# Factor of batch 1 spread in fp32, last output products in two-bank tiles, copies of q of batch 1 by ScalarE

## The chip, the core and the metric

The kernel runs on one core of one Trainium2 chip. A core has five engines that run their own instruction streams: TensorE (PE, matrix products; its weight loads are shown apart as PEld), VectorE (DVE), ScalarE (ACT), GpSimd (POOL) and SyncE (SP). POOL and SP mostly start transfers here. SBUF is the working memory, PSUM the small memory [...] into which TensorE writes. The metric is the device time of one execution in microseconds (us); a smaller one is better.

## What is computed

Two layers follow each other, for 8 batches of 576 positions:

```
kv  = sum over s of k[b,h,s,:] v[b,h,s,:]          # 64 x 64 for each of 8 heads
o   = q @ kv                                        # 576 x 64 for each head
x   = o / sqrt(mean over the head's 64 of o*o + 1e-6) * g_norm
h   = relu(x @ w_in)                                # 512 -> 1024
c   = conv_w[0]*h[s-1] + conv_w[1]*h[s] + conv_w[2]*h[s+1]
out = (h * sigmoid(c)) @ w_out                      # 1024 -> 512
```

q, k, v, the weights and the output are fp32 in memory; most of the work is in bf16. The factor `1/sqrt(...)` is one number for each batch, head and position, so it has to be *spread* over the 64 partitions of its head before it can multiply `o`.

## The kernel before

**An order written out by hand.** The kernel defines about forty small operations, each a Python function. The string `ORDER` lists calls of them (`hm.1.6` is `hm(1, 6)`), and each engine gets its instructions in exactly that order, each behind the one before it (the loop at the end adds an ordering for every engine). Semaphores between the engines come from the data and the buffers alone. So nothing is scheduled at run time: an engine that waits holds up all that stands behind it in its own stream.

**The operations, by the letters used in the order.** A number after the letters is the batch `b`, or the pair of batches `p`, or the stage of the convolution `c`.

- `Lq`, `Lk`, `Lv`, `Lw`: POOL starts the loads of q, k, v and of `w_out`. `ws`: DVE writes `w_in`, times g_norm, as bf16.
- `qt` (`qs` for batch 0): TensorE transposes q into PSUM; `qc` (`qd`): the copy of it to SBUF as `qT`, 128 x 1152 for half a batch. `kv`, `kvc`: the products k'v and their copies.
- `ot.b.t`: the product `o` of head pair t; `sq`: ScalarE squares it; `oc`: a copy of it in fp32.
- The norm of batch 0 takes another way (`on`, `nl`, `nx`, `mu0`). For the others: `ss` sums the squares, `ln` and `ex` (ScalarE, log then exponential) make the factor `rs` in fp32, 128 x 288. Batch 1 is normed alone, then batches 2 and 3 together, 4 and 5, 6 and 7.
- For batches 1, 2 and 3 the factor is spread by TensorE: `sl` (DVE, four instructions, lines 535 to 538) splits the fp32 factor into bf16 parts that stand in different partitions, and `sp.b.t` multiplies them by a matrix of zeros and ones, `spread` (written by `cs` on DVE), which adds the parts again. `mu.b.t` (DVE) is `o` times the spread factor. For batches 4 to 7 it is spread by transfers over DRAM: `rw`, `rr` (SP) and `mr` (DVE).
- `hm.b.f` (eight products of 128 x 288): one 128-wide slice of `h`; `re`: relu by ScalarE. `cv`, `sv`, `mv`: the convolution of two slices of batch 0 by TensorE. `ta`, `ad`: the convolution by DVE; `sg`: sigmoid by ScalarE; `mg`: h times gate by DVE.
- `om.p.m` (eight products of 128 x 512): 128 rows of the output; `ea`: the copy by ScalarE; `st`: SP stores it.
- `wu.n`, `wa.n`: n products of zeros by zeros that keep TensorE busy.

**PSUM.** Two pools: `ps_a` has three tiles of two banks each (`hm`, `ot`, `qt`, `sp`, `cv`, and the last `om`, which is computed in two halves), `ps_b` two tiles of one bank (`om`, `kv`, `ss`, `wu`). A product waits until the earlier contents of its tile have been read.

**Who copies.** `copy` (line 235) gives a copy to DVE or to ScalarE: `qc` goes to DVE unless its name is in the list `ON_ACT`.

Of the kernel before, what the change touches and what calls it, by code (L numbers as in the profile page):

```python
# [51 lines left out]
FP32 = mybir.dt.float32  # L52
# [10 lines left out]

ONES, KEEP, XB, RD, SQO, PW, ON_ACT, ON_DVE = ({0: (0, 1, 2, 3)}, ((0, 2), (0, 3)), (), (), (), (), ('oc.0.0',), ())

ORDER = """
cvq wu.11 qs.0.0 qd.0.0 cvk kv.0.0.1 kvc.0.0.1.0 kvc.0.0.1.1 cs wa.3 ot.0.0 oc.0.0 qs.0.1 kv.0.1.1 sq.0.0 wa.2
on.0.0 nl.0.0 kvc.0.1.1.1 kvc.0.1.1.0 qd.0.1 qs.0.2 wu.1 kv.0.2.1 qd.0.2 kvc.0.2.1.0 kvc.0.2.1.1 ot.0.1 wu.1  # L70
ot.0.2 sq.0.2 oc.0.1 nx.0.0 sd.0.1 wu.3 on.0.2 nl.0.2 Lq.1 nx.0.2 kv.0.3.1 mu0.0.0 kvc.0.3.1.0 kvc.0.3.1.1
qs.0.3 qd.0.3 on.0.1 nl.0.1 wa.4 ot.0.3 sq.0.3 mu0.0.2 cx cz ws.0 nx.0.1 mu0.0.1 wu.2 on.0.3 nl.0.3 nx.0.3
mu0.0.3 wu.5 hs.0.0 hs.0.1 hm.0.0 hm.0.1 re.0.1 re.0.0 Lk.1.0 Lv.1.0 Lk.1.1 ws.1 hm.0.2 hm.0.3 Lv.1.1 Lw Lq.2
Lk.2.2 re.0.2 ws.2 di.1 hm.0.7 qt.1.0 re.0.7 re.0.3 di.0 hm.0.6 re.0.6 hm.0.4 kv.1.0.2 qc.1.0 kvc.1.0.2.1
kvc.1.0.2.0 cm ta.0.2 re.0.4 hm.0.5 re.0.5 ot.1.1 sq.1.1 oc.1.1 ta.0.3 Lv.2.2 ad.0.1 qt.1.1 ot.1.0 oc.1.0
kv.1.2.2 kvc.1.2.2.1 cv.0.1 kvc.1.2.2.0 ta.0.6 qc.1.1 sq.1.0 ot.1.3 sq.1.3 ot.1.2 ta.0.7 ad.0.3 sq.1.2 wu.4
ss.1 oc.1.3 ln.1 ex.1 ta.0.4 sl.1 cv.0.0 ta.0.5 sv.0.0 sv.0.1 oc.1.2 wu.10 sp.1.0 mu.1.0 sp.1.1 sp.1.3 mu.1.1
mu.1.3 qt.2.1 sp.1.2 mu.1.2 qt.2.0 sg.0.1 sg.0.3 mg.0.3 qc.2.0 ad.0.2 hm.1.6 hm.1.7 re.1.6 qc.2.1 sg.0.2
mg.0.2 hm.1.4 hm.1.5 re.1.7 kv.2.0.4 re.1.5 kvc.2.0.4.0 kvc.2.0.4.1 re.1.4 hm.1.0 mg.0.1 ta.1.6 ta.1.7 mv.0.0
Lq.3 Lk.3.2 Lv.3.2 Lq.4 Lk.4.2 ot.2.3 oc.2.3 sq.2.3 hm.1.3 re.1.3 qt.3.1 re.1.0 ot.2.0 ot.2.1 oc.2.0 oc.2.1  # L80
ad.1.3 qc.3.1 sq.2.0 hm.1.2 ot.2.2 sq.2.1 qt.3.0 oc.2.2 sq.2.2 re.1.2 kv.3.0.4 hm.1.1 kvc.3.0.4.1 kvc.3.0.4.0
ot.3.2 re.1.1 ta.1.4 mv.0.1 ta.1.5 ad.1.2 qc.3.0 ot.3.1 sq.3.2 oc.3.2 sq.3.1 om.0.1 ta.1.2 ot.3.0 Lv.4.2
oc.3.1 ot.3.3 qt.4.1 sq.3.0 ss.2 ta.1.3 ad.1.1 sq.3.3 ss.3 qc.4.1 ea.0.1 ta.1.0 ta.1.1 ln.2 qt.4.0 qc.4.0
om.0.0 ex.2 om.0.3 sl.2 oc.3.3 oc.3.0 ea.0.0 ea.0.3 Lq.5 Lk.5.2 Lv.5.2 Lq.6 sp.2.0 sp.3.2 mu.2.0 sp.2.2 mu.3.2
mu.2.2 kv.4.0.4 sg.1.1 sg.1.3 sp.2.1 sp.2.3 om.0.2 sp.3.0 mu.2.3 mu.2.1 mg.1.1 kvc.4.0.4.1 mu.3.0 sp.3.3
hm.2.0 hm.2.3 sg.1.2 re.2.0 kvc.4.0.4.0 mu.3.3 Lk.6.2 mg.1.3 re.2.3 ea.0.2 sp.3.1 mu.3.1 hm.2.2 mg.1.2 re.2.2
ad.1.0 ot.4.0 sq.4.0 hm.3.2 oc.4.0 qt.5.1 kv.5.0.4 qc.5.1 re.3.2 sg.1.0 hm.3.3 kvc.5.0.4.0 ot.4.3 qt.5.0
re.3.3 ta.2.2 sq.4.3 hm.3.1 Lv.6.2 oc.4.3 kvc.5.0.4.1 mg.1.0 re.3.1 ot.4.1 qc.5.0 sq.4.1 oc.4.1 hm.3.0 hm.2.6
ta.2.3 ad.2.1 Lq.7 ot.5.2 re.3.0 re.2.6 hm.2.1 hm.2.7 oc.5.2 sq.5.2 re.2.1 ot.4.2 re.2.7 hm.3.6 st.0.2 oc.4.2
sq.4.2 hm.3.7 ta.2.0 ta.2.1 re.3.6 re.3.7 ot.5.3 hm.3.5 ot.5.0 sq.5.3 st.0.3 st.0.0 st.0.1 Lk.7.2 Lv.7.2  # L90
oc.5.3 re.3.5 sq.5.0 ss.4 ot.5.1 hm.2.4 sq.5.1 ss.5 oc.5.0 om.0.7 ad.2.0 re.2.4 ta.2.6 ta.2.7 ad.2.3 hm.3.4
ln.3 ex.3 oc.5.1 hm.2.5 re.3.4 rw.3 ea.0.7 re.2.5 st.0.7 qt.6.0 qt.6.1 sg.2.3 rr.4.0 om.0.4 ea.0.4 om.0.8
ea.0.8 ta.2.4 ta.2.5 ad.2.2 qc.6.1 qt.7.1 sg.2.1 kv.6.0.4 om.0.6 mr.4.0 qt.7.0 rr.4.2 qc.6.0 kvc.6.0.4.1
mr.4.2 kvc.6.0.4.0 kv.7.0.4 ea.0.6 rr.4.1 sg.2.2 mr.4.1 qc.7.0 rr.4.3 mr.4.3 qc.7.1 ot.6.2 mg.2.3 rr.5.0
rr.5.3 rr.5.2 mr.5.3 oc.6.2 sq.6.2 om.0.5 mr.5.0 hm.4.0 hm.4.6 sg.2.0 re.4.6 kvc.7.0.4.1 hm.4.7 hm.4.5 re.4.0
ea.0.5 re.4.7 re.4.5 hm.4.1 mr.5.2 rr.5.1 mr.5.1 re.4.1 st.0.5 kvc.7.0.4.0 hm.5.6 st.0.6 mg.2.1 re.5.6 ot.6.0
sq.6.0 hm.5.0 re.5.0 mg.2.2 hm.5.1 st.0.4 oc.6.0 st.0.8 re.5.1 ot.7.3 mg.2.0 ot.7.0 sq.7.3 om.1.0 ot.7.1
oc.7.3 oc.7.0 sq.7.0 ot.6.3 sq.7.1 om.1.5 oc.7.1 ta.3.0 ta.3.1 oc.6.3 ea.1.0 ot.6.1 sq.6.3 hm.5.7 hm.5.4
sq.6.1 re.5.7 ot.7.2 oc.6.1 ad.3.0 ea.1.5 sq.7.2 ss.6 st.1.0 re.5.4 hm.4.4 re.4.4 ss.7 ln.4 ex.4 hm.5.5 hm.5.2
om.1.7 re.5.5 hm.5.3 ta.3.6 ta.3.7 oc.7.2 ad.3.3 ta.3.4 hm.4.3 re.5.2 hm.4.2 om.1.2 sg.3.3 ta.3.5 ad.3.2  # L100
ea.1.7 mg.3.3 rw.4 rr.6.0 rr.6.2 st.1.5 st.1.7 rr.6.3 re.4.2 ta.3.2 re.5.3 om.1.4 ea.1.2 re.4.3 om.1.3 ea.1.4
mr.6.0 ta.3.3 sg.3.0 st.1.4 ea.1.3 mr.6.2 rr.6.1 st.1.3 om.1.8 ea.1.8 sg.3.2 ad.3.1 om.1.1 om.1.6 rr.7.3
rr.7.1 mr.6.3 mr.6.1 mg.3.0 sg.3.1 hm.6.0 hm.6.5 mg.3.2 hm.6.1 re.6.0 ta.4.0 ea.1.1 re.6.1 mr.7.1 rr.7.0
ta.4.1 mg.3.1 re.6.5 hm.6.2 hm.6.4 ad.4.0 mr.7.0 st.1.2 rr.7.2 re.6.2 hm.6.7 re.6.7 hm.6.6 ea.1.6 re.6.4
re.6.6 st.1.1 ta.4.4 st.1.6 hm.6.3 re.6.3 om.2.2 om.2.7 mr.7.3 ta.4.5 mr.7.2 ea.2.7 hm.7.4 sg.4.0 re.7.4
hm.7.2 ad.4.2 sg.4.2 re.7.2 hm.7.0 hm.7.6 re.7.0 ta.4.2 st.1.8 ea.2.2 hm.7.3 st.2.7 re.7.3 st.2.2 re.7.6
hm.7.5 hm.7.7 re.7.5 hm.7.1 mg.4.0 ta.4.3 ad.4.1 ta.4.6 ta.4.7 ad.4.3 om.2.6 ta.5.2 mg.4.2 ta.5.3 ad.5.1
om.2.4 sg.4.1 sg.4.3 ea.2.6 st.2.6 ea.2.4 om.2.3 ea.2.3 sg.5.1 re.7.1 om.2.1 st.2.3 ta.5.4 om.2.8 mg.4.3
ea.2.1 ea.2.8 ta.5.5 mg.4.1 om.3.0 ea.3.0 st.2.1 st.3.0 ad.5.2 sg.5.2 ta.5.0 ta.5.1 ad.5.0 om.2.0 ea.2.0
st.2.4 re.7.7 st.2.0 ta.5.6 ta.5.7 om.3.3 sg.5.0 ea.3.3 om.3.2 mg.5.2 om.2.5 ea.3.2 ad.5.3 sg.5.3 ea.2.5  # L110
mg.5.0 st.3.2 mg.5.1 om.3.1 ea.3.1 st.3.3 st.3.1 mg.5.3 om.3.4 ea.3.4 st.2.5 st.3.4 st.2.8 om.3.8 ea.3.8
st.3.8 om.3.5 ea.3.5 om.3.6 ea.3.6 st.3.6 st.3.5 om.3.7 ea.3.7 st.3.7
"""


# [1 line left out]
def kernel(  # L117
# [25 lines left out]
    consts = pool("consts", 1)  # L143
# [3 lines left out]
    ps_a = pool("ps_a", BUFS["a"], space=PSUM)  # L147
# [5 lines left out]
    def load(name, b, h0=0, n=H):  # L153
        src = {"q": q, "k": k, "v": v}[name]
        if (name, b) not in qkv:
            qkv[name, b] = loads.tile([PS, H, R * D], BF16, name=name + "_sb", bufs=BUFS[name])
        nc.gpsimd.dma_start(  # L157
            out=qkv[name, b][:, h0:h0 + n, :],
            in_=src[b, h0:h0 + n].rearrange("h (p r) d -> p h (r d)", r=R))
# [82 lines left out]
    T = {}  # L242
# [29 lines left out]
    idv = ident.rearrange("p (t g c) -> p t g c", t=NT, g=4)  # L272
# [215 lines left out]
    def rows_of(g):  # L488
        return 32 * len(pairs_of(NORM[g][0]))
# [50 lines left out]
    @op  # L540
    def sp(b, t):
        g = NG[b]
        n = rows_of(g)
        bi = NORM[g].index(b)
        ps = ps_a.tile([P, 2, 512], FP32, name="sp_ps", tag="a")
        T["sp", b, t] = ps
        for e in range(2):
            nc.tensor.matmul(
                ps[:, e, :HS], spread[:n, t * 4 + 2 * bi + e, :, :].rearrange("p i d -> p (i d)"), T["w", g],
                start=True, stop=True)  # L550
# [140 lines left out]
    @op  # L691
    def om(p, m):
        h = T["h", p].rearrange("p f b s -> p f (b s)")
        if f"om.{p}.{m}" == LAST:
            ps = ps_a.tile([P, 2, 512], FP32, name="om2_ps", tag="a")
            parts = [(ps[:, i, :D_model // 2], slice(i * D_model // 2, (i + 1) * D_model // 2)) for i in range(2)]
        else:
            ps = ps_b.tile([P, D_model], FP32, name="om_ps", tag="b")
            parts = [(ps, slice(0, D_model))]
        T["om", p, m] = parts  # L700
        for to, cols in parts:
            for f in range(NF):
                nc.tensor.matmul(to, h[:, f, m * P:(m + 1) * P], w_out_sb[:, f, cols],  # L703
                                 start=(f == 0), stop=(f == NF - 1))
# [37 lines left out]
    for ins in list(nc.cur_bb.bb.instructions):  # L742
        e = ins.engine
# [36 lines left out]
```

## Time and profile before

| | us |
|---|---|
| median of three runs (189.17 to 190.07) | 189.31 |
| the profiled execution | 190.19 |
| span of the profiled execution (first to last instruction) | 187.9 |
| TensorE busy in it, 1787 products | 178.5 (95%) |
| DVE busy, 324 instructions | 159.4 (85%) |
| ACT busy, 233 instructions | 150.2 (80%) |
| POOL busy, 42 instructions | 29.3 (16%) |

Matrix products overlap, so a busy TensorE is not one at its peak; how long a product keeps the next one away is read from the distance of the starts of two neighbours, not from its own duration. Work of one engine hides behind that of another wherever no one waits for it. A line number such as L548 is that of the kernel before, as printed above.

### The profile page before, as it was taken

The page shows a single profiled execution, that of the slowest core. Times are in us where ns is not written, and L with a number is a line of the kernel's source. Part 1 is how long each engine was busy: PE and PEld are TensorE (multiplying, and loading weights), DVE is VectorE, ACT ScalarE, POOL GpSimd, SP SyncE. Part 2 cuts the span into 40 slices and gives each one's busy share as a digit, 9 for nine tenths or more (in the row PEclk, how much of TensorE's full clock was granted, in tenths as well). Part 3 has the DMA queues.
Part 4 walks back from the last instruction along what each step waited for, and adds up shares of the span by engine and source line. Part 5 has one row for each costly group of instructions (what it writes and reads, how often), then busy time and mean ns, then how long its engine had stood idle before and what let it go on. Part 6 is the DMA issues. An engine that isn't in the chain of part 4 may idle for free.

```text
span 187.9 us, 4432 instructions
## 1 busy us (share of the span) xinstructions
PE 178.5 (95%) x1787; PEld 108.0 (57%) x1787; DVE 159.4 (85%) x324; ACT 150.2 (80%) x233; POOL 29.3 (16%) x42
## 2 busy tenths in 40 slices
PE   7899998999899999999999999999999999999991
PEld 2444774566555577765566656664467675444451
DVE  4678599898999899999998899999899999999200
ACT  2449689949999899999999999999977496667431
POOL 7994405013052301400000000000000000000000
PEclk9999999999999999999999999999999999999999
DMA  6999999999999999998366531028485220233454
GB/s 147 183 265 332 203 205 204 206 202 203 204 204 203 207 200 238 265 205 128 118 178 196 198 131 61 0 89 262 161 232 178 98 81 3 108 128 129 166 195 167
DMA packets 30876, 32.35 MB, mean 172 GB/s; under 512 B 1776, under 2 KB 25864, under 8 KB 30856
## 3 DMA queue, kind: packets, MB, share of 16 engines
q0 software_dynamic: 20176, 17.01, 54.6%
q1 hardware_dynamic: 10472, 14.76, 23.2%
q10 hardware_dynamic: 208, 0.29, 0.6%
q8 instruction: 14, 0.23, 0.5%
q14 instruction: 6, 0.05, 0.1%
HBM read 37.24 MB, written 9.73 MB: 250 GB/s over the span
## 4 chain that ended last, share of the span: by engine, by line
PE 47%; ACT 25%; DMA 9%; DVE 8%; SPq 4%; issue 2%; POOL 2%; ACTq 0%; POOLq 0%; DVEq 0%
PE om_ps L703 20%; PE h_ps L595 19%; ACT h L608 7%; DMA rb<-scr 6%; ACT sq L435 6%; ACT o L239 5%; SPq L571 3%; DMA v_sb<-in_v_dram 3%; PE kv_ps L319 2%; DVE h L649 2%; ACT L232 2%; ACT row L710 2%; DVE xT L580 2%; PE qt_ps L361 1%; DVE xT L554 1%
## 5 line engine op out<-in xcount | busy, mean ns | idle before, releaser
L595 PE MATMUL h_ps<-xT,w_in_sb 128*128 128x288 bf16 x512 | 68.4, 286 | 1.7 <-DVE xT L580 0.6
L703 PE MATMUL om_ps<-w_out_sb,h 128*128 128x512 bf16 (+1 forms) x296 | 64.4, 373 | 0.0
L595 PEld LDWEIGHTS <-w_in_sb 128*128 128x128 bf16 x512 | 49.3, 98 | 18.6 <-issue 4.1
L703 PEld LDWEIGHTS <-h 128*128 128x128 bf16 x296 | 28.5, 98 | 31.7 <-DVE h L649 0.3
L608 ACT ACTIVATE h<-h_ps 128x576 bf16<-128x576 f32 x64 | 40.1, 656 | 7.0 <-PE h_ps L595 6.6
L628 DVE TENSOR_SCALAR side<-h,cw 128x576 bf16<-128x576 bf16 (+1 forms) x92 | 38.2, 427 | 1.0
L643 ACT ACTIVATE tap<-tap 128x1152 bf16<-128x1152 bf16 (+1 forms) x23 | 34.1, 1496 | 2.3 <-DVE tap L637 2.3
L710 ACT ACTIVATE row<-om_ps 128x512 f32<-128x512 f32 (+1 forms) x37 | 21.5, 586 | 14.9 <-PE om_ps L703 13.6
L637 DVE TENSOR_TENSOR tap<-tap,side 128x1150 bf16<-128x1150 bf16 (+1 forms) x23 | 22.4, 973 | 0.8
L649 DVE TENSOR_TENSOR h<-h,tap 128x1152 bf16<-128x1152 bf16 (+1 forms) x23 | 21.6, 962 | 0.6 <-ACT tap L643 0.6
L636 DVE TENSOR_TENSOR tap<-tap,side 128x1150 bf16<-128x1150 bf16 (+1 forms) x23 | 22.1, 961 | 0.0
L435 ACT ACTIVATE sq<-o_ps 128x576 bf16<-128x576 f32 x31 | 19.7, 662 | 1.9 <-PE o_ps L393 1.9
L239 ACT ACTIVATE o<-o_ps 128x576 f32<-128x576 f32 x29 | 18.5, 657 | 1.8 <-PE o_ps L393 1.8
L628 DVE TENSOR_SCALAR tap<-h,cw 128x576 bf16<-128x576 bf16 (+1 forms) x46 | 19.3, 421 | 0.0
L580 DVE TENSOR_TENSOR xT<-o,rb 128x576 bf16<-128x576 f32 x16 | 12.0, 755 | 2.2 <-DMA rb<-scr 2.1
L237 DVE COPY qT<-qt_ps 128x1152 bf16<-128x1152 bf16 x14 | 10.5, 753 | 3.0 <-PE qt_ps L361 3.0
L728 PE MATMUL wu_ps<-zeros 128*128 128x512 bf16 x37 | 11.6, 454 | 1.2 <-DVE zeros L184 1.2
L157 POOL DMA_DIRECT2D q_sb<-in_q_dram x10 | 7.6, 756 | 33.1 <-PE qt_ps L361 32.2
L393 PE MATMUL o_ps<-qT,kvbd 128*128 128x512 bf16 x32 | 11.7, 379 | 0.0
L157 POOL DMA_DIRECT2D k_sb<-in_k_dram x11 | 9.1, 828 | 11.7 <-PE kv_ps L319 9.0
L361 PEld LDWEIGHTS <-q_sb 96*64 96x64 bf16 x336 | 8.3, 110 | 3.8 <-issue 3.4
L361 PE MATMUL qt_ps<-ident,q_sb 96*64 96x96 bf16 x336 | 9.6, 207 | 0.5 <-DVE xT L554 0.2
(72 smaller groups left out, 126.6 us busy)
## 6 DMA issues: line engine op xcount, KB each, us to landing
out_dram<-row SPq DMA_DIRECT2D x35, 256.0 KB, 2.3
rb<-scr SPq DMA_DIRECT2D x32, 144.0 KB, 3.5
q_sb<-in_q_dram POOLq DMA_DIRECT2D x7, 576.0 KB, 12.1
k_sb<-in_k_dram POOLq DMA_DIRECT2D x6, 576.0 KB, 11.8
v_sb<-in_v_dram POOLq DMA_DIRECT2D x6, 576.0 KB, 15.2
w_stage<-in_moe_w_in_dram POOLq DMA_DIRECT2D x2, 512.0 KB, 6.7
w_stage<-in_moe_w_in_dram POOLq DMA_DIRECT2D x1, 1024.0 KB, 9.5
w_out_sb<-in_moe_w_out_dram POOLq DMA_DIRECT2D x1, 1024.0 KB, 17.8
```

Source lines behind the costliest of these rows:

```text
L239: nc.scalar.activation(to, fr, AX.Copy)
L361: nc.tensor.transpose(ps[i * D:(i + 1) * D, tt, r * PS:(r + 1) * PS], q_sb[:, 2 * (2 * u + tt) + i, r * D:(r + 1) * D], ident[:PS, :PS])
L435: nc.scalar.activation(to, fr, AX.Square)
L595: nc.tensor.matmul(ps[:, e, :HS], w_in_sb[:, t, f * P:(f + 1) * P], x[:, t, e * HS:(e + 1) * HS], start=(t == 0), stop=(t == NT - 1))
L608: nc.scalar.activation(h_tile(b // 2)[:, f, b % 2, :].rearrange("p (e n) -> p e n", e=2), T["hm", b, f][:, :, :HS], AX.Relu)
L628: nc.vector.tensor_scalar_mul(tap[m][:, f % 2, :, :].rearrange("p b s -> p (b s)"), h_tile(p)[:, f, bs, :].rearrange("p b s -> p (b s)"), ...
L636: nc.vector.tensor_add(tap[:, :, 1:], tap[:, :, 1:], side[:, 0, :, :S - 1])
L637: nc.vector.tensor_add(tap[:, :, :S - 1], tap[:, :, :S - 1], side[:, 1, :, 1:])
L643: nc.scalar.activation(tap, tap, AX.Sigmoid)
L649: nc.vector.tensor_mul(h, h, T["tap", c, j])
L703: nc.tensor.matmul(to, h[:, f, m * P:(m + 1) * P], w_out_sb[:, f, cols], start=(f == 0), stop=(f == NF - 1))
L710: nc.scalar.activation(T["os", p, m][:, cols], fr, AX.Copy)
```

## The change

Three lists and the order change, and two operations follow them.

- Batch 1's factor is no longer split. Its `sl` is gone, and `sp.1.t` multiplies the fp32 factor by an fp32 matrix of zeros and ones, `spread32`, with two fp32 products of 128 x 288 for each t. `spread32` (128 x 1024 fp32) is written by POOL, ahead of the load of `w_out`. Batches 2 and 3 keep the split.
- Eight `om` tiles among the last (of the pairs 2 and 3) go to the pool of two-bank tiles `ps_a` instead of `ps_b`, and use one bank of theirs.
- The two copies of the transposed q of batch 1, `qc.1.0` and `qc.1.1`, go from DVE to ScalarE.
- The order is a new one throughout. There are 26 products of zeros ahead of the first `hs` (32 before) and 17 after it (14 before). All other operations are the same, and the loads stand in the same order on POOL.

```diff
-..., ON_ACT, ON_DVE = (..., ('oc.0.0',), ())
+..., ON_ACT, ON_DVE, F32, OM_A = (..., ('oc.0.0', 'qc.1.0', 'qc.1.1'), (), (1,), ((2, 6), (2, 8), (3, 2), (3, 0), (2, 1), (3, 5), (3, 7), (3, 6)))
...
+    spread32 = consts.tile([P, NT * 2, 2, D], FP32, name="spread32") if F32 else None
+
     @op
     def Lw():
+        if F32:
+            nc.gpsimd.tensor_copy(
+                spread32.rearrange("p (t e) i d -> p t (e i) d", t=NT),
+                idv[:, :, 0, 0:4].unsqueeze(3).to_broadcast([P, NT, 4, D]))
         nc.gpsimd.dma_start(out=w_out_sb, in_=moe_w_out.rearrange("(f p) m -> p f m", p=P))
...
     def sp(b, t):
...
+        if g in F32:
+            for e in range(2):
+                nc.tensor.matmul(
+                    ps[:, e, :HS], spread32[:n, 2 * t + e].rearrange("p i d -> p (i d)"), T["rs", g],
+                    start=True, stop=True)
+            return
...
     def om(p, m):
...
+        elif (p, m) in OM_A:
+            ps = ps_a.tile([P, 2, 512], FP32, name="om2_ps", tag="a")
+            parts = [(ps[:, 0], slice(0, D_model))]
```

The order from the copies of q of batch 1 to its first `hm`, before:

```
qt.1.0 re.0.7 re.0.3 di.0 hm.0.6 re.0.6 hm.0.4 kv.1.0.2 qc.1.0 kvc.1.0.2.1 kvc.1.0.2.0 cm ta.0.2 re.0.4 hm.0.5 re.0.5
ot.1.1 sq.1.1 oc.1.1 ta.0.3 Lv.2.2 ad.0.1 qt.1.1 ot.1.0 oc.1.0 kv.1.2.2 kvc.1.2.2.1 cv.0.1 kvc.1.2.2.0 ta.0.6 qc.1.1
sq.1.0 ot.1.3 sq.1.3 ot.1.2 ta.0.7 ad.0.3 sq.1.2 wu.4 ss.1 oc.1.3 ln.1 ex.1 ta.0.4 sl.1 cv.0.0 ta.0.5 sv.0.0 sv.0.1
oc.1.2 wu.10 sp.1.0 mu.1.0 sp.1.1 sp.1.3 mu.1.1 mu.1.3 qt.2.1 sp.1.2 mu.1.2 qt.2.0 sg.0.1 sg.0.3 mg.0.3 qc.2.0
ad.0.2 hm.1.6
```

and after:

```
hm.0.6 re.0.6 qt.1.1 ta.0.2 qc.1.1 qt.1.0 qc.1.0 re.0.5 wu.2 hm.0.7 kv.1.0.2 cs ta.0.3 ad.0.1 ta.0.6 re.0.7 di.1
hm.0.4 ta.0.7 ad.0.3 kvc.1.0.2.1 kvc.1.0.2.0 re.0.4 wu.4 ot.1.0 oc.1.0 sq.1.0 kv.1.2.2 ot.1.1 kvc.1.2.2.1 kvc.1.2.2.0
sq.1.1 wu.4 ot.1.2 ta.0.4 sq.1.2 ot.1.3 sq.1.3 wu.5 ss.1 oc.1.2 oc.1.3 cv.0.1 ln.1 ex.1 ta.0.5 ad.0.2 wu.2 sp.1.3
mu.1.3 oc.1.1 sp.1.0 mu.1.0 sv.0.1 cv.0.0 sp.1.1 sp.1.2 mu.1.1 sg.0.3 sv.0.0 mu.1.2 sg.0.2 qt.2.0 qt.2.1 mv.0.0
qc.2.1 qc.2.0 hm.1.2
```

The writing of the bf16 matrix, `cs` (three DVE instructions, L276 to L278), stands in the start before and among the convolution of batch 0 after. The first `om` stands behind all of `hm.1` before (`om.0.1`), and after it (`om.0.3`) between `ot.2.2` and `oc.2.2`, ahead of `hm.1.5`.

## The prediction

> **What bounds the kernel now.** I read the page first, then the table by stages, then TensorE's timeline, and last the waits. The page puts PE at 95%, DVE at 85% and ACT at 80% of the span, an average that says little. The table below cuts the time from TensorE's first `hm` product (18.03) to its last, at the first `hm` of batch 1, just after the last of them (55.10, in the first `om`), and at the starts of `hm.4.0` and `hm.6.0`. Columns: stretch, length, then busy time (and count) of PE, PEld, DVE, ACT, POOL, the granted clock, DMA share, GB/s.
>
> ```profile
> 18.03:39.20 21.17, 20.07 (x260) 13.17 (x259) 17.13 (x40) 18.02 (x34) 4.46 (x5) 1.00 1.29 204
> 39.20:55.10 15.90, 14.91 (x226) 10.22 (x227) 15.23 (x33) 13.01 (x24) 4.74 (x6) 1.00 1.32 204
> 55.10:101.34 46.24, 45.88 (x650) 29.84 (x648) 43.63 (x70) 45.28 (x69) 5.09 (x6) 1.00 1.05 195
> 101.34:136.38 35.04, 34.66 (x231) 20.56 (x230) 33.25 (x47) 34.22 (x51) 0.00 (x0) 1.00 0.39 131
> 136.38:184.03 47.65, 47.22 (x281) 27.26 (x279) 37.98 (x80) 29.75 (x44) 0.00 (x0) 1.00 0.37 131
> ```
>
> TensorE is nearly full in every row, ACT too from 55 to 136 (79.5 of 81.3 us), DVE in the second row. In the last row only TensorE is. So the end is TensorE's work plus its stalls, and ACT decides in the middle. Real stalls come from distances of starts, in TensorE's timeline around batch 1's factor (start, length, instruction):
>
> ```profile
> 32.34 0.43 PE L500 MATMUL ss_ps<-sq,sel 128*32 128x288 bf16 x8
> 32.85 0.90 PE L670 MATMUL cv_ps<-h,dg 128*128 128x288 bf16 x6
> 33.59 2.32 PE L728 MATMUL wu_ps<-zeros 128*128 128x512 bf16 x10
> 35.81 1.49 PE L548 MATMUL sp_ps<-wparts,spread 128*128 128x288 bf16 x6
> ...
> 39.20 1.14 PE L595 MATMUL h_ps<-xT,w_in_sb 128*128 128x288 bf16 x8
> ...
> 148.23 8.12 PE L595 MATMUL h_ps<-xT,w_in_sb 128*128 128x288 bf16 x64
> 156.18 27.81 PE L703 MATMUL om_ps<-w_out_sb,h 128*128 128x512 bf16 x136
> ```
>
> The unstalled spacing is 0.124 us for 128 x 288 ((156.18 - 148.23)/64) and 0.216 for 128 x 512 (a tile of eight takes 1.73; the fifteen whole tiles and two halves of the last row make 27.7 of its 27.81, so the end has no stall). With these spacings the first stretch is 13.5 us of useful products, 1.0 of `sp.1`, 3.0 of zeros (14 x 0.216) and 3.7 of stalls; the second has 2.8 us of stalls, the third 2.9, the fourth 1.4, the last 0.7. Some 0.1 us at each change of kind is in these and stays.
>
> The ten products of zeros stand where TensorE waits for the split on DVE:
>
> ```profile
> 33.83 0.31 DVE L535 CAST hi<-rs 128x288 bf16<-128x288 f32 x1 [0.39 <-ACT rs L526]
> 34.17 0.52 DVE L536 SCALAR_TENSOR_TENSOR rs<-hi,na,rs 128x288 f32<-128x288 bf16 x1
> 34.73 0.31 DVE L537 CAST hi<-rs 128x288 bf16<-128x288 f32 x1
> 35.08 0.52 DVE L538 SCALAR_TENSOR_TENSOR wparts<-hi,nb,rs 128x288 bf16<-128x288 bf16 x1
> ```
>
> From `rs` (33.79) to `wparts` (35.60) 1.8 us pass: that is the wait to be removed.
>
> [...] No fp32 product of this size is in the trace (the one transpose, L260, is 25 columns). [...] The trace has one case, 133 ns for L260's weights against 98 for bf16 ones. [...]
>
> **The change, part by part.**
>
> *fp32 products.* [...] With 0.05 us left open for each, 4.4: I take +3.4. [...] `mu.1` on DVE (0.75 each, 3.0 in all) no longer paces them.
>
> *Split.* Four DVE instructions, 1.66 us busy, are gone. Before, TensorE reached `sp` at 35.81.
>
> *Copies of q.* Two DVE copies of 753 ns leave; ACT gets two of 128 x 1152 out of PSUM. No row shows this; 128 x 576 copies follow each other at 0.545 (two in 1.09 in the chain), the 1152-wide sigmoid takes 1.16. I take 1.1 each, 2.2 (2.1 to 2.4). What stands behind them on ACT is `re.0.5`, `re.0.7`, `di.1`, the `kvc` and all squares, so `ss.1` waits for them. From `re.0.6` (TensorE, with six `hm.0` done, releases it at about 24.1) ACT then has 4 relus, 4 squares and 3 copies (11 x 0.545 = 6.0), four `kvc` (4 x 0.275 = 1.1), `di.1` (0.98), the two copies (2.2) and `ln`, `ex` (1.0): 11.3, ending at 35.4. So `sp.1.3` starts at 35.4, 0.4 earlier than before, although the split is gone: ACT's new work takes its place.
>
> *Sum of the first stretch after.* 13.5 useful + 4.4 + zeros 17 x 0.216 = 3.7 + stalls. The walk (`sp.1.3` 35.4; two `sp`, `cv.0.0` 0.73, two `sp`: 40.5; `mu.1.2` done at 41.4) gives `hm.1.2` at about 41.6: stalls of 2.0 instead of 3.7. Net +2.4 on 39.20.
>
> *Zeros ahead of `hs`.* Six fewer, 1.3 us; worth nothing, because this stretch follows the loads: the chain has 5.34 us of the load of v, up to 11.03. `cs` (1.58 us of DVE) leaves the start: there it stood while TensorE waited for v until 8.93. It goes to where DVE has 17.13 of 21.17 busy. If that cover were gone it would cost 1.6.
>
> *POOL's copy.* 128 x 1024 fp32, an estimate of 1 to 1.5 us, ahead of the loads of `w_out` and of q, k, v of batch 2. POOL waits 32.2 us in all for `qt`; `w_out` landed at 32.9 (15.08 + 17.8) and is first read at 53.85; v of batch 2 landed at 41.8 (22.65 + 19.1) and is first read at 43.73, so 2 us are to spare. Hidden; without that margin it would be 1 to 1.5 us on TensorE. [...]
>
> *Order from 39 to 55.* Before, TensorE lost 2.8 us here to ACT and to tiles, with nothing else to issue. After, `om.0.3` (1.73 us, one `ps_b` tile) stands among `hm.1`, between `ot.2.2` and `ot.2.0`, where ACT has to read several tiles. I count 1.6 back of 2.8. So at 55 TensorE is +0.8, with DVE 3.2 us lighter (1.66 + 1.51) and ACT level (its free 2.9 us of this stretch absorb the copies).
>
> *From 55 on.* The same operations in another order. In the chain before, the first `rr.4` waited behind a store (`st.0.7`, for an `ea`), and `hm.6.0` waited 0.56 for `mr`. After, `rr.6.3` still stands behind `st.1.4` on SP, behind a sigmoid of ACT; TensorE arrives there later and so waits less: -0.4. Everything else I put at even.
>
> *Two-bank tiles.* The last 27.81 us held no stall, so they can remove none: 0. An `om` in `ps_a` occupies a tile for 1.73 + 0.6; at worst it delays one `hm.7` by 0.3.
>
> Sum: +2.4 - 1.6 - 0.4 = +0.4. Against the profiled execution, 190.19 (span 187.9 and 2.3 around it), that is 190.6; on the median, 189.31, it is 189.7. Half a per cent of this kernel, 0.95 us, is about what a measurement can tell from no change; the forecast is inside it.
>
> **Rivals.**
>
> 1. *The stalls go (faster).* DVE is 3.2 us lighter just where it held 15.23 of 15.90, and an order around that may pack TensorE closer. If the second stretch gets back 2.1 of 2.8, the third 1.2 of 2.9 and the rest 0.6 of 2.1, the sum is 2.4 - 2.1 - 1.2 - 0.6 = -1.5: 187.8. For it: every one of these stalls is short and has a filler somewhere. Against it: from 55 to 136 ACT is 98% full, and the new order gives it no less to do.
>
> 2. *The fp32 products cost more (slower).* Place: the four `sp.1` tiles, with nothing else for TensorE but `cv.0.0`. [...] 1.7 more than assumed: +2.1, 191.4[...]. It decides from about 0.62 us a product on (+0.95 = 0.4 + 8 x 0.07). [...] Against: weight loads of the bf16 products hide behind the one before.
>
> 3. *ACT is the bound (slower).* The copies' 2.2 us shift all of ACT up to 121, where its Ln of batches 6 and 7 starts, and with it `rr.6` and `hm.6.0`. ACT has 2.9 us free in the second stretch, which speaks against it; if half of that can't be used, +1.1 on top: 190.8.
>
> 4. *It does nothing of what it says:* the split was hidden by zeros and other products anyway. That is already in the forecast; the result is the same time.
>
> **How the numbers follow.** Forecast 0.34, rival 1 0.30, rival 2 0.22, rival 3 0.14. The likeliest case alone holds 188.9 to 190.4. The range goes from rival 1's 187.8 to 192.2, which holds rival 3 and rival 2 up to products of 0.8 us (0.4 + 8 x 0.25 = 2.4 on 189.31 is 191.7, with 0.5 for the rest); beyond it and below 187.8 lie 2 in 10. Faster by over 0.5%: 0.30. Slower: most of rival 2, half of rival 3 and a little of the forecast, 0.34. Within: 0.36.
>
> **What would show it.** In the timeline after: starts of neighbouring `sp.1` products 0.5 to 0.6 apart ([...]over 0.62: rival 2); `sp.1.3` at about 35.4 with ACT unbroken before it; `hm.1.2` at about 41.6; ACT's 1152-wide copies at 1.1; POOL's copy under 1.5 and no later k or v wait on TensorE. In the table by stages: stalls of about 1 us instead of 2.8 in the stretch of `hm.1` (less than 0.7 there and less than 2 up to `hm.4.0`: rival 1); ACT's free time from 55 to `hm.6.0` (1.8 us before; rival 3 is right if it stays near that and the stretch still begins late). The prediction is wrong if TensorE's distance from `hm.4.0` to the end, 82.7 us, changes by over 1 us, since I put the late order at even.

## The result and the profile after

| | before | after |
|---|---|---|
| median (6 executions of each, on one chip) | 189.69 | 191.85 |
| lowest to highest | 188.82 to 190.48 | 191.20 to 193.26 |
| the profiled execution | 190.19 | 192.28 |
| its span | 187.9 | 190.4 |

The ratio is 1.0126, with a 95% interval of 1.0086 to 1.0167: slower by about 2.4 us; the medians differ by 2.2. (A ratio is taken from the executions within 1.5% of a kernel's fastest one and is not the quotient of the medians, here 1.0114, which are of all executions.) The forecast was +0.4 us, inside what can't be told from no change. The value lies in the predicted range, and the forecast itself was wrong. That it lies in the range is luck: the upper end, 192.2, was drawn for dearer fp32 products or a late ScalarE, and what was missed lies elsewhere.

The table by stages of the kernel after, cut at the same places as that of before (first `hm`; first `hm` of batch 1; last `hm` of batch 1; `hm.4.0`; `hm.6.0`; end of TensorE's work). Columns as before: stretch, length, busy time (and count) of PE, PEld, DVE, ACT, POOL, granted clock, DMA share, GB/s.

```profile
19.12:42.60 23.48, 22.93 (x270) 15.32 (x268) 17.39 (x35) 20.10 (x36) 4.18 (x5) 1.00 1.30 204
42.60:56.23 13.63, 13.63 (x229) 10.09 (x226) 13.15 (x31) 11.55 (x21) 3.69 (x5) 1.00 1.31 203
56.23:103.24 47.01, 46.18 (x652) 30.05 (x651) 43.90 (x71) 46.21 (x70) 5.68 (x8) 1.00 0.98 182
103.24:138.81 35.57, 34.46 (x231) 20.67 (x230) 33.56 (x47) 34.15 (x51) 0.00 (x0) 1.00 0.43 138
138.81:186.13 47.32, 47.12 (x281) 27.18 (x279) 37.38 (x80) 29.67 (x44) 0.00 (x0) 1.00 0.37 135
```

The second and third rows don't hold the same products in both kernels, because `om.0.3` has moved; together they do. So the 2.5 us between the spans are split like this (distances of starts, from TensorE's timelines):

| | before | after | difference | predicted |
|---|---|---|---|---|
| start to the first `hm` | 18.03 | 19.12 | +1.09 | 0 |
| to the first `hm` of batch 1 | 21.17 | 23.48 | +2.31 | +2.4 |
| to `hm.4.0` | 62.14 | 60.64 | -1.50 | -1.6 |
| to `hm.6.0` | 35.04 | 35.57 | +0.53 | 0 |
| to the end of TensorE's work | 47.65 | 47.32 | -0.33 | -0.4 |
| last copies and stores | 3.85 | 4.31 | +0.46 | 0 |

Three rows are right to 0.1 us, and two are not: the start, and the stretch from `hm.4.0` to `hm.6.0`. (The -0.4 of the prediction is a wait at the third product of `hm.6.0`, so it belongs to the row that begins with this tile.) Without the last row the differences make +2.1, and by this much the two profiled executions differ in time (192.28 - 190.19): about the forecast's +0.4 and the two misses, +1.09 and +0.53.

The last row is in the span and not in the time. It comes with the fp32 products: from TensorE's last product to the end of the span pass 4.3 us in the kernel after and in experiments 1 and 3, which have them, and 3.9 us in the profiles of all other kernels. But the time exceeds the span by 1.8 to 1.9 us in these three and by 2.3 in the others. The reason is not shown.

**The start.** The table by stages again, for 8 to 17 us, of the kernel after:

```profile
8.00:11.00 3.00, 2.01 (x31) 0.88 (x29) 1.50 (x5) 1.18 (x2) 2.65 (x5) 1.00 1.25 182
11.00:14.00 3.00, 2.05 (x42) 1.27 (x43) 2.83 (x9) 2.65 (x5) 2.78 (x5) 1.00 1.17 307
14.00:17.00 3.00, 3.00 (x10) 0.92 (x7) 1.83 (x6) 1.31 (x2) 2.37 (x4) 0.50 1.03 366
```

and of the kernel before:

```profile
8.00:11.00 3.00, 2.27 (x42) 1.28 (x41) 2.50 (x5) 1.93 (x3) 3.00 (x4) 1.00 1.28 191
11.00:14.00 3.00, 2.74 (x44) 1.39 (x46) 2.15 (x5) 1.45 (x3) 3.00 (x6) 1.00 1.14 299
```

The numbers to look at are the one behind the comma (TensorE's busy time) and the third from the end (granted clock). With six products of zeros fewer ahead of the first `hm`, TensorE is busy for 2.0 of 3 us in two stretches, and then its clock is granted at 0.50 for the third; before, it is 1.00 there too. What that does to it is in TensorE's timeline of the kernel after:

```profile
14.24 2.34 PE L746 MATMUL wu_ps<-zeros 128*128 128x512 bf16 x5
16.37 0.26 PE L401 MATMUL o_ps<-qT,kvbd 128*128 128x64 bf16 x1
```

Five products of zeros take 2.13 us from their first to the next instruction; the five at 18.04 in the same kernel take 1.08. Up to there the kernel after isn't late: the last product k'v of batch 0, `kv.0.3`, starts at 13.54, and at 13.60 before. The dip isn't in every execution: four of the six of the kernel after have a mean clock of 0.978 to 0.991 and a median of 192.3 us, the two others (0.996 and 1.00) took 191.3 and 191.4. So +1.09 is what it cost in the profiled one.

**The factor of batch 1.** TensorE's timeline of the kernel after (an fp32 product is recorded as two pairs of weight load and matmul, so x8 are four products):

```profile
36.57 2.18 PE L558 MATMUL sp_ps<-rs,spread 128*128 128x288 f32 x8 [0.17 <-ACT rs L535]
38.69 0.90 PE L685 MATMUL cv_ps<-h,dg 128*128 128x288 bf16 x6
39.43 2.10 PE L558 MATMUL sp_ps<-rs,spread 128*128 128x288 f32 x8
...
42.60 3.11 PE L610 MATMUL h_ps<-xT,w_in_sb 128*128 128x288 bf16 x24
```

The eight products take 2.12 + 2.03 = 4.15 us, 0.52 each. They start 17.45 us after the first `hm` and as soon as ACT has the factor (`[0.17 <-ACT rs L535]`). The four lines of the split on DVE are gone from this stretch.

**From `hm.4.0` to `hm.6.0`.** The factors of batches 4 and 5 come by sixteen transfers (`rr.4`, `rr.5`) that SP issues behind the one that writes the factor (`rw.3`, `scr<-rs`). SP's timeline before:

```profile
89.13 0.33 SPq L562 DMA_DIRECT2D scr<-rs  x1
90.70 0.34 SPq L721 DMA_DIRECT2D out_dram<-row  x1
91.13 12.61 SPq L571 DMA_DIRECT2D rb<-scr  x16
```

and after:

```profile
91.03 0.33 SPq L577 DMA_DIRECT2D scr<-rs  x1
91.39 2.09 SPq L739 DMA_DIRECT2D out_dram<-row  x2
93.58 6.24 SPq L586 DMA_DIRECT2D rb<-scr  x8
99.92 0.54 SPq L739 DMA_DIRECT2D out_dram<-row  x1
100.56 5.98 SPq L586 DMA_DIRECT2D rb<-scr  x8
```

Before, one store stands between `rw.3` and the sixteen, which then follow in a row; the last is issued 14.6 us after `rw.3` has begun (103.74 - 89.13). After, two stores stand ahead of them and a third (`st.0.4`) between, and the last is issued 15.5 us after `rw.3` (106.54 - 91.03). DVE's timeline after shows the `mr` of batch 5 waiting for these transfers, where before the waits are 0.41 and 0.22, and TensorE's shows who pays; before, the same tile, `hm.5.6`, waits 0.19:

```profile
107.83 0.76 DVE L595 TENSOR_TENSOR xT<-o,rb 128x576 bf16<-128x576 f32 x1 [0.68 <-DMA rb<-scr]
109.57 1.43 DVE L595 TENSOR_TENSOR xT<-o,rb 128x576 bf16<-128x576 f32 x2 [0.98 <-DMA rb<-scr]
```

```profile
110.38 2.13 PE L610 MATMUL h_ps<-xT,w_in_sb 128*128 128x288 bf16 x16 [0.64 <-DVE xT L595]
```

This is no chance of one execution. In the experiments below the way from `hm.4.0` to `hm.6.0` takes 35.2 to 35.9 us in the profiles of 1, 2, 5, 6 and 10, which have this late order, and 34.6 to 35.0 in those of 3, 4, 7, 8 and 9, which have that of before.

### The profile page after: what moved, and what is told of

The parts are those of the page before. It is cut to its first block, busy times and chain, and to the rows that moved or that the text cites. A ratio compares the mean times of both kernels' runs of the same rounds, so it can differ in the third digit from the quotient of the medians.

```text
span 190.4 us, 4444 instructions
## 1 busy us (share of the span) xinstructions
PE 180.3 (95%) x1792; PEld 110.3 (58%) x1792; DVE 156.9 (82%) x318; ACT 151.6 (80%) x235; POOL 28.8 (15%) x43
## 4 chain that ended last, share of the span: by engine, by line
PE 41%; DVE 27%; ACT 17%; DMA 5%; POOL 3%; issue 2%; SPq 2%; DVEq 0%; ACTq 0%; POOLq 0%
PE h_ps L610 18%; PE om_ps L721 15%; DVE side L643 7%; DVE tap L652 5%; DVE h L664 4%; DVE tap L651 4%; DVE tap L643 3%; DMA v_sb<-in_v_dram 3%; ACT sq L444 3%; ACT tap L658 3%; ACT h L623 3%; ACT o L241 3%; PE sp_ps L558 2%; PE wu_ps L746 2%; DMA rb<-scr 2%
## 5 line engine op out<-in xcount | busy, mean ns | idle before, releaser
L610 PE MATMUL h_ps<-xT,w_in_sb 128*128 128x288 bf16 x512 | 66.9, 286 | 1.0 <-DVE xT L595 0.6
L728 ACT ACTIVATE row<-om_ps 128x512 f32<-128x512 f32 (+1 forms) x37 | 21.0, 586 | 12.1 <-PE om_ps L721 10.3
L746 PE MATMUL wu_ps<-zeros 128*128 128x512 bf16 x42 | 14.4, 477 | 1.2 <-DVE zeros L186 1.2
L569 DVE TENSOR_TENSOR xT<-o,sp_ps 128x576 bf16<-128x576 f32 x12 | 8.7, 750 | 4.1 <-PE sp_ps L558 3.3
L159 POOL DMA_DIRECT2D k_sb<-in_k_dram x11 | 8.4, 763 | 15.7 <-PE kv_ps L328 11.8
L239 DVE COPY qT<-qt_ps 128x1152 bf16<-128x1152 bf16 x12 | 8.9, 751 | 1.2 <-PE qt_ps L370 1.1
## 6 DMA issues: line engine op xcount, KB each, us to landing
w_out_sb<-in_moe_w_out_dram POOLq DMA_DIRECT2D x1, 1024.0 KB, 18.6
```

The lines of the kernel that those rows point to most:

```text
L610: nc.tensor.matmul(ps[:, e, :HS], w_in_sb[:, t, f * P:(f + 1) * P], x[:, t, e * HS:(e + 1) * HS], start=(t == 0), stop=(t == NT - 1))
L728: nc.scalar.activation(T["os", p, m][:, cols], fr, AX.Copy)
L746: nc.tensor.matmul(ps, zeros[:, 0, :], zeros.rearrange("p t c -> p (t c)"), start=True, stop=True)
```

## The experiments

My theory after the result: the loss has two main parts, a start in which TensorE's clock falls, which the prediction had at nothing, and fp32 products that cost more than the split that they replace, which it had in its sum. The rivals: the copies on ACT, the two-bank tiles, or the order itself. All were timed in five rounds beside the kernel before. Line numbers in these kernels differ by a few from those printed above.

**1. More zeros at the start of the kernel after** (eight products of 128 x 512).

```diff
-... wu.1 kv.0.1.1 ... wu.1 kv.0.2.1 ... ot.0.2 on.0.1 sq.0.2 ...
+... wu.4 kv.0.1.1 ... wu.3 kv.0.2.1 ... ot.0.2 wu.1 on.0.1 wu.2 sq.0.2 ...
```

> The changed kernel with eight more products of zeros ahead of the first hm: wu.4 and wu.3 instead of two wu.1, a wu.1 before and a wu.2 after on.0.1, all where TensorE waits for loads or copies. Nothing else differs. Theory 'clock': the change took six zeros from the start, TensorE's clock fell to half between about 14 and 17 us (the five zeros of wu.5 took 2.13 us instead of 1.08), and all behind it is 1.1 us late; with the zeros back wu.5 takes 1.1, the first hm starts near 18.0 instead of 19.12, and the time falls by 0.8 to 1.2 us, to about 0.5 to 0.7% above the kernel before. Theory 'fp32': the start is no matter, later stalls absorb it, and the time stays within 0.3 us of the changed kernel, 1.1 to 1.3% above before.

Measured: 191.02 us, ratio to before 1.0071 [1.0041, 1.0101], where the unchanged kernel after has 1.0126. TensorE is busy for 3.00 and 2.77 us of the two stretches, the clock stays at 1.00, from 14 to 17 us too:

```profile
8.00:11.00 3.00, 3.00 (x48) 1.39 (x45) 1.84 (x5) 1.79 (x3) 3.00 (x5) 1.00 1.30 193
11.00:14.00 3.00, 2.77 (x44) 1.33 (x37) 2.79 (x11) 2.50 (x5) 3.00 (x6) 1.00 1.14 325
```

The first `hm` is at 17.38 instead of 19.12, and `hm.4.0` and `hm.6.0` are still 1.3 and 1.5 earlier than in the kernel after. None of the eight executions has a mean clock under 0.994. So about 0.55 percentage points of the 1.26% are the start (an estimate from the two intervals: 0.05 to 1.05), and eight products that compute nothing (1.7 us of TensorE) win them back. Not all of it is the clock: 17.38 is also earlier than the 18.03 of before. In the profiles of experiments 5, 6 and 10, which have the same start, the first `hm` comes at 17.8 to 18.1.

**2. The split back in the kernel after**, directly behind the convolution `ad.0.2` on DVE.

```diff
-F32 = (1,)
+F32 = ()
-... ln.1 ex.1 ta.0.5 ad.0.2 wu.2 sp.1.3 ...
+... ln.1 ex.1 ta.0.5 ad.0.2 sl.1 wu.2 sp.1.3 ...
```

> The changed kernel with batch 1's factor split again (sl.1 on DVE behind ad.0.2, bf16 products by spread, no spread32 on POOL), all else as changed. Theory 'fp32': the eight fp32 products cost 8 x (0.52 - 0.124) = 3.2 us of TensorE; the split costs 1.75 us of waiting and the four mu then pace the stage (3.0 us), so the first hm of batch 1 starts 0.5 us earlier and TensorE has the rest as stalls: the time falls by 0.5 to 1 us. Theory 'clock': the start is as cold as in the changed kernel, the first hm still near 19.1, and at most 0.5 us is gained: still 1% above before.

Measured: 191.44 us, 1.0050 [1.0015, 1.0085]. In its profiled execution the clock is at 0.50 from 11.8 to 18.6 us, and again from 39.1 to 42.5, right behind 1.87 us in which TensorE waits for the split, so its stages are not compared; experiment 5 has them. The three of its ten executions with the lowest mean clock (0.968 to 0.973) took 193.0 to 193.4 us, the three with the highest (0.997 to 0.999) 189.5 to 190.4; over all ten the quotient of the medians is 1.007.

**3. The fp32 products alone in the kernel before** (no `sl.1`; its order else kept, the ten zeros `wu.10` too; `spread32` on POOL comes with them).

```diff
-F32 = ()
+F32 = (1,)
-... ta.0.4 sl.1 cv.0.0 ta.0.5 ...
+... ta.0.4 cv.0.0 ta.0.5 ...
```

> The kernel before with the fp32 spread of batch 1 alone: no sl.1, spread32 on POOL, its own order otherwise, wu.10 kept. In that order the first sp waits for sv.0.0 to release its tile at 35.7, so removing the split frees nothing. Theory 'fp32': sp.1 still starts at 35.8, the stage takes 4 x 1.04 and two qt instead of 3.4 us, and the time rises by 1.5 to 2 us (0.8 to 1.1%). If the products hide behind mu: less than 0.5 us.

Measured: 192.84 us, 1.0162 [1.0133, 1.0190], the most expensive single part by far. TensorE's timeline:

```profile
34.33 2.32 PE L742 MATMUL wu_ps<-zeros 128*128 128x512 bf16 x10
36.64 3.15 PE L554 MATMUL sp_ps<-rs,spread 128*128 128x288 f32 x12
```

and ACT's, at the same time:

```profile
34.09 0.44 ACT L531 ACTIVATE rs<-rs 128x288 f32<-128x288 f32 x1
34.55 1.28 ACT L230 ACT_TABLE_LOAD   x1
35.84 1.19 ACT L689 ACTIVATE sq<-cv_ps 128x576 bf16<-128x576 f32 x2
```

The factor is there at 34.53, yet the first `sp` starts at 36.64 and not earlier than before (35.81), for two reasons that don't need the split: TensorE has the zeros until 36.5, and the PSUM tile that `sp` takes is that of `cv.0.0`, which ACT reads behind its table load (the first of the two sigmoids ends at about 36.5). In this order the split was hidden completely. So taking it away brings nothing, the products cost their 3.1 us more, and the first `hm` of batch 1 is 3.3 later (42.50, 39.20 before).

**4. The copies of q of batch 1 on ACT, alone in the kernel before.**

```diff
-ON_ACT = ('oc.0.0',)
+ON_ACT = ('oc.0.0', 'qc.1.0', 'qc.1.1')
```

> The kernel before with the two copies of q of batch 1 given to ScalarE and nothing else. Theory 'clock' and 'fp32': ScalarE has 3 us free between 18 and 39 us, DVE gains 1.5: within 0.5 us of before. Theory 'ACT': the copies stand ahead of the squares of batch 1, so its factor and all of ScalarE come 1 to 2 us later: 0.5 to 1% slower.

Measured: 190.91 us, 1.0063 [1.0042, 1.0083]. ACT's timeline has the copy at its price, and TensorE's the wait behind it:

```profile
30.76 1.11 ACT L237 ACTIVATE qT<-qt_ps 128x1152 bf16<-128x1152 bf16 x1
```

```profile
31.92 0.19 PE L397 MATMUL o_ps<-qT,kvbd 128*128 128x64 bf16 x1 [1.22 <-ACT qT L237]
```

Everything from `ss.1` (33.66, 32.34 before) to the first `hm` of batch 1 (40.52, 39.20) is 1.3 later: ACT paces this stretch, and two copies of 1.1 us stand in the way of the squares.

**5. Both: more zeros at the start, and the split instead of fp32, in the kernel after.**

> The changed kernel with both repairs: the eight zeros at the start and the bf16 split of batch 1's factor. If the cold start and the fp32 products are two separate costs, their gains add: 1.26% less 0.55 less 0.76 leaves the kernel at about the time of before (-0.2 to +0.3%). If both are absorbed by the same later stall, it stays near the better of the two alone, +0.5%.

Measured: 190.57 us, 1.0023 [0.9992, 1.0053]. With the warm start the split is 0.48 points better than fp32 (1.0071), without it 0.76 (1.0126 to 1.0050). That the two gains add up fits their intervals, which are wide: each of these differences is uncertain by 0.4 to 0.5 (estimated from the intervals). What is left over the kernel before, 0.23%, can't be told from zero. It stands for the new order, the copies on ACT and the two-bank tiles together.

**6. The same with the copies of q back on DVE.**

```diff
-ON_ACT = ('oc.0.0', 'qc.1.0', 'qc.1.1')
+ON_ACT = ('oc.0.0',)
```

> As after_warm_split, and the two copies of q of batch 1 on DVE again; what is left of the change is the order and the two-bank tiles. Theory 'ACT': ScalarE's chain to the factor (measured 25.8 to 36.4 us without a gap) gets 2.1 us shorter, the first sp comes 1 to 2 us earlier, and the time falls by 0.5 to 1 us below after_warm_split, below the kernel before. Otherwise within 0.3 us of after_warm_split.

Measured: 193.36 us, 1.0161 [1.0132, 1.0191], 1.4% above experiment 5. The expectation that ACT's relief helps fell. The order is written for a DVE without these copies: DVE is now late with the convolution, and the split stands behind it. DVE's timeline, and TensorE's:

```profile
37.03 0.30 DVE L540 CAST hi<-rs 128x288 bf16<-128x288 f32 x1
```

```profile
38.84 1.14 PE L559 MATMUL sp_ps<-wparts,spread 128*128 128x288 bf16 x4 [3.85 <-DVE wparts L543]
```

The factor was ready at 35.02, the split began at 37.03, and TensorE stood still for 3.85 us (1.87 in experiment 5). Behind this wait its clock fell too, as the table by stages shows:

```profile
38.80:42.21 3.41, 3.37 (x14) 1.93 (x14) 1.61 (x3) 0.75 (x2) 0.00 (x0) 0.50 1.32 203
```

Counted from the first `hm`, the first `sp` comes 1.3 us later than in experiment 5, and from there to the first `hm` of batch 1 it takes 4.64 us instead of 3.49: nearly half of this loss falls into the dip. All five executions have a mean clock of 0.982 to 0.991. So in the order of after the copies on ACT are needed, although in that of before they cost 0.63%.

**7. The two-bank tiles alone in the kernel before.**

```diff
-OM_A = ()
+OM_A = ((2, 6), (2, 8), (3, 2), (3, 0), (2, 1), (3, 5), (3, 7), (3, 6))
```

> The kernel before with the eight last output tiles in two-bank tiles and nothing else. All theories: its last 27.7 us hold no stall, so the time stays within 0.3% of before; over 0.5% slower would mean that the h products of batch 7 wait for these tiles.

Measured: 190.56 us, 1.0025 [1.0002, 1.0048]. No gain, at most half a per cent lost. TensorE's timeline shows one new stall, 0.60 us at 163.19: an `om` that waits until ACT has read the tile of an `hm`.

**8. The kernel before with 26 zeros ahead of the first `hs`** (the first part of an `hm` of batch 0), as in the kernel after.

```diff
-... wa.3 ... wa.2 ... wu.3 ... wa.4 ...
+... wa.1 ... wa.1 ... wu.1 ... wa.3 ...
```

> The kernel before with 26 instead of 32 zeros ahead of the first hm (wa.1, wa.1, wu.1 and wa.3 for wa.3, wa.2, wu.3 and wa.4). Theory 'clock': TensorE's clock drops between 10 and 18 us in at least some executions, the first hm starts up to 1 us later, and the time rises by 0.3 to 0.6%. Otherwise, as the prediction had it: no difference.

Measured: 190.27 us, 1.0009 [0.9981, 1.0036], no difference in the median. The profiled execution (191.54) shows the same dip, earlier and longer, in its table by stages (0.69 from 8 to 11 us, then):

```profile
11.00:14.00 3.00, 2.94 (x31) 1.51 (x28) 1.67 (x5) 0.60 (x1) 3.00 (x5) 0.50 1.11 300
```

Its first `hm` is at 19.77. The median hides that there are two kinds of executions. Eight of the 14 have a mean clock of 0.972 to 0.991 and a median of 191.3 us; the six others (0.996 to 1.00) have one of 189.8. Of the 43 executions of the kernel before beside them only three are at 0.991 or under. So six zeros fewer, with nothing else changed, make the dip frequent, and where it comes it costs about 1.5 us; they don't decide whether it comes.

**9. The start of the kernel after, warm, in front of the order of before.** This was meant as a version that beats both. `cs`, the writing of the bf16 matrix, has to go behind the copies `kvc.1.0.2`.

> The kernel before (split on DVE, copies on DVE, its own order from the first hs on), but with the start of the kernel after and its warm zeros ahead of hs; the writing of the bf16 matrix, cs, moves behind the copies kvc.1.0.2. Theory that the start is a term of its own which is carried to the end: the first hs at 17.4 instead of 18.03, first hm of batch 1 at about 38.6 to 39.0, the time 0.2 to 0.4% under that of the kernel before. Rival, that cs costs 1.58 us once it has left the start, where DVE then holds the split up: first hm of batch 1 at 39.5 to 40.3, the time 0.2 to 0.7% above it.

Measured: 190.45 us, 1.0055 [1.0031, 1.0079]. The rival was right. DVE's timeline:

```profile
25.22 1.23 DVE L276 COPY spread<-bg 128x2048 bf16<-128x2048 bf16 x1
...
34.73 0.30 DVE L540 CAST hi<-rs 128x288 bf16<-128x288 f32 x1
```

`cs` pushes the convolution from 24.99 to 26.36 and the split from 33.83 to 34.73; the first `hm` of batch 1 comes at 40.03 instead of 39.20, although the first `hm` of all was 0.23 earlier. In the kernel after, `cs` stands in the same place, and the copies of q have left DVE there: experiment 6, where they come back, speaks for the two moves belonging together. The warm start gains little here, since half of `hm.0` waits for the last part of `w_in` (0.42 at 22.30).

**10. The split earlier on DVE, ahead of the convolution `ta.0.5`, `ad.0.2`,** in the kernel of experiment 5.

```diff
-... ex.1 ta.0.5 ad.0.2 sl.1 wu.2 ...
+... ex.1 sl.1 ta.0.5 ad.0.2 wu.2 ...
```

> The kernel after with the warm start and the split on DVE directly behind the exponential, ahead of the convolution of batch 0 (ta.0.5 and ad.0.2), instead of behind it. Theory that the split is cheap where DVE is free when the factor is ready: the split's wparts at 1.8 to 2.3 us behind rs, first sp product at about 37.0, first hm of batch 1 at 39.8 to 40.3 (41.3 with fp32), the time 0.3 to 0.6% under the one with the warm start and the fp32 products. Rival, that the convolution is then late and stops batch 0's part: the gain of the first hm is lost by the first hm of batch 2 and the time is the same.

Measured: 192.18 us, 1.0115 [1.0070, 1.0159]. Both expectations fell. DVE's timeline:

```profile
35.46 0.31 DVE L540 CAST hi<-rs 128x288 bf16<-128x288 f32 x1 [3.50 <-ACT rs L531]
...
39.44 2.74 DVE L565 TENSOR_TENSOR xT<-o,sp_ps 128x576 bf16<-128x576 f32 x4
```

DVE has waited 3.50 us for the factor with the convolution behind the split; then the convolution stands ahead of the `mu.1`, which begin at 39.44 (38.26 in experiment 5). From the first `hm` of all to the first of batch 1 it is 24.41 us, 23.21 in experiment 5. The place of four short instructions in DVE's order is worth 1.2 us.

**11. The late order alone:** the kernel before up to `hm.4.0`, then the order of after, with the two-bank tiles.

> The kernel before up to the first product of hm.4.0, and from there the order of the kernel after (with its two-bank tiles; split on DVE and copies of q on DVE as before). Theory that the late order itself is worse by what the two profiles show from hm.4.0 on (+0.5 up to hm.6.0, -0.3 after it): hm.4.0 at 101.3, hm.6.0 at 136.6 to 137.0, the time 0.1 to 0.3% above the kernel before. Rival, that the late order is as good and the kernel after lost 0.5 us there only because its transfers of the factor (rr.4, rr.5) start later against hm.4.0 than before: hm.6.0 at 136.0 to 136.5, the time within 0.1% of the kernel before or under it.

Measured: 190.75 us, 1.0054 [1.0024, 1.0085], above both expectations. The seam between the orders costs by itself: `ot.7.0` follows its copies at once and waits 1.32 us for them, so that `hm.4.0` is at 102.60. Behind it the late order isn't slower: 34.46 us to `hm.6.0` (35.04 before, 35.57 after; one `ot`, about 0.25 us, less stands in this stretch) and 45.03 from there to the end of the next-to-last output tile (45.70 and 45.41). Here the transfers begin as early as before (SP issues fourteen in a row from 90.67), and `hm.5.6` and the `om` behind the gate don't wait; a wait of 0.64 for ACT stands ahead of them instead. That speaks for the late transfers and against the order of the products, but since TensorE comes 1.3 later, it also waits less: the run doesn't settle it.

**12. The kernel of experiment 5 up to `hm.4.0`, then the order of before.**

> The kernel after with the warm start and the split on DVE behind ad.0.2, up to hm.4.0, and from there the order of the kernel before (one-bank tiles). Theory that the late order is worse in itself: 0.1 to 0.3% under the same kernel with the late order of after (which took 1.0023 of the time before), so between 0.9990 and 1.0015. Rival, that the late start of the transfers rr.4 and rr.5 decides, which this kernel keeps: no gain, 1.002 or more.

Measured: 197.60 us, 1.0421 [1.0372, 1.0470]. It tells nothing of the late order: at the seam TensorE waits 2.76 us for the copies ahead of `ot.6.2`, then has its clock at 0.50 from 105.6 to 109.1, and six of the transfers `rr.5` stand behind a store, with DVE idle for 4.30 us for what they bring.

Both runs were badly made in this respect: the order was cut where the two halves hold different operations in flight, and TensorE waited 1.32 and 2.76 us at the seams.

## Where the prediction was right and where it was wrong, step by step

**fp32 products: right.** Predicted 0.55 us each, measured 0.52, which is 4.2 times the 0.124 of a bf16 product of the same size. The 0.55 was the author's estimate: nothing in the profile of before shows an fp32 product of this size. Rival 2 needed 0.62.

**Split, copies, walk to the first `hm` of batch 1: right.** `sp.1.3` was put 17.4 us behind the first `hm` and came at 17.45; the stretch was put 2.4 longer and is 2.31 longer. ACT's copies were put at 1.1 each, and two took 2.15. That ACT's new work takes the place of the split is in the trace after (the products start 0.17 behind the factor, with ACT unbroken from 25.20 on); that the copies on ACT delay this stretch was tested in the order of before only (experiment 4, +1.3 us).

**Zeros ahead of `hs`, "worth nothing": wrong, and the largest miss.** I looked at what the zeros delay and not at what they keep up. The stretch follows the loads only as long as TensorE runs at its full clock: from 14.24 us to the first `hm` TensorE's timeline of the kernel after shows no wait. Its clock there was 0.50 over the whole of 14 to 17 us and 0.94 in the three after it. From 8 to 14 us, ahead of the dip, TensorE was busy for 68% of the time; in experiment 1, where it was busy for 96%, the clock stayed at 1.00. By what rule the clock falls is not shown. Term predicted 0; measured +1.09 in the profile, 0.55 points between experiment 1 and the kernel after. That fewer zeros bring the dip is shown by experiments 1 and 8: it is in none of eight executions with eight zeros more, and the mean clock is low in eight of 14 of the kernel before with six fewer.

**Order from 39 to 55, -1.6, and from there even: the sum right, the parts not.** At `ss.2` the kernel after has done one output tile (1.73 us) more, so 17.33 - 1.73 = 15.60 stand against 17.75: 2.15 came back. Up to `hm.4.0`, 0.65 of it was lost again, among it waits of 0.26 at `hm.2.0` and 0.28 at `sp.3.0`. That the sum comes out at -1.5 is in part luck.

**"After, `rr.6.3` still stands behind `st.1.4` ...: -0.4": right; "Everything else I put at even": wrong.** The 0.56 at `hm.6.0` did go, and for the reason given: the last transfer that it needs is issued at 133.8 in both profiles, and TensorE arrives at 138.81 instead of 136.38. But I followed one of the groups of transfers only. `rr.4` and `rr.5` have two stores ahead of them, where before there was one, and one in their middle, and the wait is now at `hm.5.6`, the first of batch 5 (0.64 for 0.19), with 0.37 at an `om` behind the gate: +0.53 instead of 0. That `hm.5.6` waits for these transfers is in the trace. That the stores are the cause was argued from SP's timelines, and experiment 11 supports it without settling it.

**POOL's copy: right in size (1.05 us for 1 to 1.5, the author's estimate, as the profile of before has no such copy) and hidden.** One DVE instruction took longer beside it, as the timelines of POOL and DVE of the kernel after show:

```profile
14.36 1.05 POOL L306 CAST spread<-ident 128x1024 f32<-128x1024 bf16 x1
```

```profile
12.67 0.74 DVE L489 TENSOR_TENSOR xT<-o,o 128x576 bf16<-128x576 f32 x1
14.75 1.29 DVE L489 TENSOR_TENSOR xT<-o,o 128x576 bf16<-128x576 f32 x1 [0.19 <-ACT o L474]
```

The same instruction took 0.55 us longer where it started inside POOL's copy; it ends 0.63 after it. Experiment 1 has it again (1.28 us, ending 0.62 after the copy); in experiments 2 and 5, whose kernels have no such copy, this instruction takes 0.76. In the kernel after, DVE then waits 1.29 us for another engine, so nothing comes of it. Why it took longer is not shown.

**Two-bank tiles, 0, at worst 0.3: no gain, as put, but not the stall that was named.** Experiment 7 has +0.25% [0.02, 0.48] and a stall of 0.60 us, in which an `om` waits for the tile of an `hm` and not an `hm` for that of an `om`. In the order of after TensorE's timeline shows no wait for ACT from `hm.6.0` on.

**The rivals.** Rival 1 fell, stalls went in one stretch and came in others. Rival 2 fell by its own threshold. Rival 3 has its mechanism in experiment 4, but in the order of after the copies are the better choice (experiment 6). Rival 4 holds for the split in the order of before (experiment 3). None of them had the clock at the start or the transfers of batches 4 and 5, and these two put the result on the slower side.

**What the loss is made of.** Of the 1.26%, about 0.55 is the start (experiment 1), about 0.48 the fp32 products in the place of the split (1 against 5), and the rest, 0.23 [-0.08, 0.53], the new order with the copies and the tiles. The first two are uncertain by 0.5 and 0.4. The fp32 products are no miss of the forecast, which had them at their price; it had hoped to win it back. No version of these beats the kernel before.

## What to carry to other kernels

Products of zeros in a stretch that waits for loads may hold the clock up (here, from 14 to 17 us, it was 1.00 with eight more of them and 0.50 without, experiment 1): before counting their removal as free, look at TensorE's busy share in the stretches around them, not only at who waits for them. Ask of a removed step what else ends at the same time (here zeros and a table load), since a step that was hidden gives nothing back while its replacement costs its full price (3.1 us in experiment 3). And when an order changes, follow every queue of small transfers, with the stores among them, and not only the one that the old chain of waits shows. Where executions of one kernel differ in their mean clock, read them in two groups: a median can hide what one group loses (experiment 8).

## What was not expected of the hardware

- TensorE's clock fell to 0.50 without a long idle time: the longest single wait from 8 to 14 us was 0.61 us, the busy share 68%; with 96% it did not fall (experiment 1). It also fell right behind single waits of 3.85 us (experiment 6) and 2.76 us (experiment 12), to 0.50 for 3.4 and 3.5 us; behind one of 1.87 us it fell in the profile of experiment 2 and not in that of experiment 5.
- An fp32 product of 128 x 128 by 128 x 288 is recorded as two pairs of weight load and matmul, 0.26 us each from start to start.
- The last 1 MB part of `w_in` took 9.5 us to land in the profile of before, and 11.0 in that of after, with the loads in the same order. In the profiles of experiments 1, 3, 5 and 9 an `hm` of batch 0 waits 0.30 to 0.49 us for this part; in those of before and after none does.
